# Moving the copy of the activation's high part from ScalarE to VectorE in the first three groups of a fused attention and SiLU-MLP kernel

## The chip, the cores and the metric

One core of a Trainium2 chip. The metric is the device time of one execution in microseconds; the kernel before has a median of 951.65 over three runs (951.26 to 954.59). TensorE multiplies, VectorE, ScalarE and GpSimd do the elementwise work, and SyncE's queue starts the transfers. In rows of a profile the engines are PE (PEld is its weight load), DVE, ACT, POOL and SP.

## The reference, cut to what matters

Windowed attention (8 batches, 8 heads, 576 positions of width 64, window 128, a bias per head that falls with distance), then an MLP on the 4608 tokens:

```python
x = attn_out.transpose(0, 2, 1, 3).reshape(B * S, H * D)     # 4608 x 512
h = x @ w_in                                                 # 512 x 2048
g = h * (1.0 / (1.0 + np.exp(-h)))                           # SiLU
return (g @ w_out).astype(np.float32)                        # 2048 x 512
```

The products have to be of float32 accuracy, so each operand is split into a high and a low part and a product is made of three matmuls: high by high, high by low, low by high.

## The kernel before, in words

**Tiling.** The 4608 tokens are nine groups of 512 (`TG`). For each group the 2048 hidden columns are 16 tiles (`NF`) of 128; tile n = 16 g + f. `gemm1(n, half)` makes `h` (128 hidden columns by 512 tokens in PSUM) in two halves of six matmuls; `gemm2(n, half)` adds the tile's share to four output tiles `o`, again six matmuls a half. In groups 0 to 2 (`OUT16 = 3`) the second product's operands are float32 in TensorE's rounded form (fp32r), from group 3 on 16-bit floats.

**The activation of a tile**, in four steps that the change is about:
- `act1` (ScalarE, L647): `gt` = tanh of the scaled `h`.
- `act2` (VectorE, L652): `gt` = (`gt` + 1) times `h`, which is twice the SiLU.
- `act3`: `gh` = the high part, a rounding copy of `gt`; on ScalarE, L660 in groups 0 to 2 and L662 after.
- `act4`: `gl` = `gt` - `gh`; on GpSimd in groups 0 to 2 (L135), but on VectorE (L137) for a group's last tile; on VectorE from group 3 on (L668).

`gemm2` of the tile reads `gh` first (two matmuls) and `gl` third. `gt`, `gh` and `gl` have two buffers each.

**What sets the order.** The program is written out in order, by a table of steps. `plan[point]` holds what is to be issued at a step; the MLP loop goes through `seq`, four steps a tile (`gemm1` twice for the tile, `gemm2` twice for the one before), and at each step issues first what the plan has (`begin`), then the matmuls. `later(k, fn, n)` puts a call k steps ahead. Every engine works through its own instructions in the order in which they were issued, so an engine that waits for one instruction's input holds all that stand behind it. A tile's `act1` comes right behind its `gemm1`; the other three are put by `later`. A group's last tile goes by `turn_over`, which issues `act2` to `act4` at once, between the pieces of the next group's input (`x_parts`, L608 on ScalarE and L610 on VectorE).

**What else runs in group 0.** The attention of the next tokens runs beside the MLP: `scores` (L431, `sp`), `row_max` on VectorE (L453, `t` and `mx`), `exps` on ScalarE (L463), `p_hi` on ScalarE (L472, `hr`), `p_lo` on VectorE (L477, `hr`), a transposing transfer, `attend` (L527, `av`), `normalize` (L545 to L554, `xs`), `x_hi` and `x_lo` (L564, L137, `x`), and `v_hi` on GpSimd (L400), `v_lo` on VectorE (L406) for the values. The scores and `av` share two PSUM buffers (tag `a`), so new scores wait for `xs` of an earlier pair and `av` for `row_max`. Group 0 alone also unpacks the weights, two tiles of them per activation tile (`w_next`): ScalarE splits (`w_split1` L730, `w_low3` L737), VectorE joins (`w_join` L742, `wm`), ScalarE makes the high part (`w_hi` L752, `w`) and GpSimd the low part (`w_lo` L135, `w`). Group 2 and the end of group 1 convert weights to 16 bits on ScalarE and VectorE (L780, L786, L792).

The lines that the change and the prediction touch: L647, L652, L660 and L135/L137 (activation), L742 and L752 (weights), L477, L406, L453, L554 (attention), L700 (`gemm2`), and the calls of `later` at L979 to L981.

Of the kernel before, what the change touches and what calls it, by code (L numbers as in the profile page):

```python
# [55 lines left out]
IN16, OUT16 = 2, 3  # L56
# [20 lines left out]
def at(p):  # L77

    if p < 2 * GT:
        return STEP * (p - 2 * GT) - 18  # L80
    if p < 4 * GT:
        return CLOSE[p - 2 * GT]
    return STEP * (p - 2 * GT) - LEAD
# [3 lines left out]
def tile_window_attention_then_silu_mlp(ctx, tc, qk, qk16, v, w_in, w_out, base8, out):  # L87
    nc = tc.nc
# [487 lines left out]
    def x_transpose(cc):  # L576
        xp = ps_of("h" if cc < 2 else "a", f"xp{cc}")
        for i in range(GT):
            nc.tensor.transpose(xp[:, i * P : (i + 1) * P], xt[i][:, cc * P : (cc + 1) * P], ident)
        nc.scalar.copy(xh[:, cc], xp)  # L580
        xps[cc] = xp

    def x_low(cc):
        nc.vector.tensor_sub(xl[:, cc], xps.pop(cc), f32(xh[:, cc]))
# [13 lines left out]
    def x_send():  # L598

        for i in [i for i in whole if i // GT <= now[0] + 1]:  # L600
            whole.remove(i)
            x_dma(i)
# [41 lines left out]
    def act1(n):  # L644
        gt = pool.tile([P, TG], F32, tag="gt", name=f"gt{n}")
        scale = 0.5 / W_SCALE if n // NF < IN16 else gsc[n // NF][:, 0:1]
        nc.scalar.activation(gt, hps[n], AF.Tanh, scale=scale)  # L647
        gact[n] = gt
# [5 lines left out]
    def act3(n):  # L654
        gt = gact[n]
        dt = F32R if n // NF < OUT16 else F16
        gh = pool.tile([P, TG], dt, tag="gh", name=f"gh{n}")
        gl = pool.tile([P, TG], dt, tag="gl", name=f"gl{n}")
        if n // NF < OUT16:
            nc.scalar.copy(gh, gt)  # L660
        else:
            nc.scalar.activation(gh, gt, AF.Copy, scale=CUT)  # L662
        gact[n] = (gh, gl, gt)
# [8 lines left out]
    def turn_over(n):  # L672

        i = (n // NF + 1) * GT
        more = n // NF + 1 < IN16
        if more:
            x_parts(i, 0)
        act2(n)
        act3(n)
        act4(n)  # L680
        if more:
            x_parts(i, 1)
            for k in range(1, GT):
                x_parts(i + k, 0)
                x_parts(i + k, 1)

    def gemm2(n, half):
        g, f = divmod(n, NF)
        for ti in (2 * half, 2 * half + 1):
            if f == 0:  # L690
                ops[ti] = psum.tile([P, DM], F32, tag="wxyz"[ti], name=f"o{g}_{ti}")
            gh, gl, _ = gact[n]
            t = slice(ti * P, (ti + 1) * P)
            if g < OUT16:
                hi, lo = weight("woh", f), weight("wol", f)
            else:
                hi, lo = w16[1, f][:, 0], w16[1, f][:, 1]
            seq = [(gh, hi), (gh, lo), (gl, hi)]
            for i, (a, w) in enumerate(seq):
                nc.tensor.matmul(  # L700
                    ops[ti], a[:, t], w, start=(f == 0 and i == 0), stop=(f == NF - 1 and i == len(seq) - 1),
                    skip_group_check=True,
                )
# [100 lines left out]
    def put(point, fn, *a):  # L804
        plan.setdefault(max(point, at(0)), []).append((fn, a))

    for p in range(NPAIR):
        i, q = divmod(p, 2)
        n = at(p)
# [65 lines left out]
    for b in range(1, NBB):  # L875

        n = at(2 * GT * (NBLK * b // GT)) + 2
# [11 lines left out]
    def later(n, fn, *a):  # L889
        put(pos[0] + n, fn, *a)  # L890
# [19 lines left out]
    def begin():  # L910
        for fn, a in plan.pop(pos[0], []):
            fn(*a)

    with tc.manual_schedule():
# [39 lines left out]
        for g in range(NG):  # L954
            now[0] = g

            seq = []
            for f in range(NF):
                n = g * NF + f
                seq += [("g1", n, 0)] + [("xt", 0, 2), ("xt", 0, 3)] * (n == 0) + [("g1", n, 1)]  # L960
                if 0 < f < NF - 1:
                    seq += [("g2", n - 1, 0), ("g2", n - 1, 1)]
            n = g * NF + NF - 1
            seq += [("g2", n - 1, 0), ("g2", n - 1, 1), ("g2", n, 0), ("g2", n, 1)]
            for k, n, half in seq:
                if k == "xt":
                    x_transpose(half)
                    x_low(half)
                    continue
                begin()  # L970
                x_send()
                if k == "g1":
                    gemm1(n, half)
                    if half == 1:
                        act1(n)
                        if n % NF == NF - 1:
                            turn_over(n)
                        else:
                            later(1, act2, n)  # L979
                            later(2, act3, n)  # L980
                            later(2, act4, n)  # L981
                else:
                    gemm2(n, half)
                    if n % NF == NF - 1:
                        store(g, 2 * half)
                        store(g, 2 * half + 1)
                if g == 0 and half == (n == 0):
                    w_next()
                pos[0] += 1
# [44 lines left out]
```

## Time and profile before

| | |
|---|---|
| median of three runs | 951.65 us (951.26 to 954.59) |
| the profiled execution | 949.61 us, its span 947.8 us |
| busy in the span | PE 97%, DVE 69%, ACT 59%, POOL 14% |
| the copy that moves (L660) | 48 times, 29.4 us on ACT, mean 613 ns |
| groups 0, 1, 2 | about 48 to 167, 167 to 274 and 274 to 380 us of the span |

Busy shares are means over stages: GpSimd works nearly only in groups 0 to 2, and ScalarE and VectorE are much fuller in group 0 than the mean says. A wait in a row is the idle time of an engine ahead of an instruction, with the instruction that ended it.

### The profile page before, as it was taken

Reading aid. Unit: us, or ns where it says so; the run is one execution under the profiler, and the core shown is the slowest. Engines: PE = TensorE matmul, PEld = TensorE weight load, DVE = VectorE, ACT = ScalarE, POOL = GpSimd, SP = SyncE. Lnnn points to the kernel's source line nnn. Section 1 sums busy time; section 2 is a strip of 40 time slices with the busy share of each in tenths; the row PEclk is TensorE's granted clock in tenths of the full one; section 3 lists DMA queues with packets and bytes.
Section 4 is the critical chain, followed back from the end, with each engine's and each line's share of the span. In section 5 each row is a group of like instructions: output and inputs, shape, how many; then the busy total and the mean of one; then the engine's idle time right before and its main releaser. Section 6 shows DMA issues by size and latency. Waiting matters only on the chain.

```text
span 947.8 us, 17110 instructions
## 1 busy us (share of the span) xinstructions
PE 921.9 (97%) x6442; PEld 574.9 (61%) x6442; DVE 655.0 (69%) x1603; ACT 558.9 (59%) x1152; POOL 133.5 (14%) x122
## 2 busy tenths in 40 slices
PE   8799999999999999999999999999999999999998
PEld 7677777777778888555545555555555545554443
DVE  4687887555778887899687778776777777743222
ACT  5678888676555674666567756555655565532222
POOL 0145665121212221000000000000000000000000
PEclk9999999999999999999999999999999999999999
DMA  9949942423277762644597765544654554421001
GB/s 277 375 119 246 272 101 67 106 65 87 65 181 200 166 142 50 156 101 101 111 244 179 221 144 132 118 112 98 139 111 104 119 142 106 87 55 56 1 1 44
DMA packets 209266, 123.28 MB, mean 130 GB/s; under 512 B 172576, under 2 KB 180768, under 8 KB 209184
## 3 DMA queue, kind: packets, MB, share of 16 engines
q1 hardware_dynamic: 209184, 122.19, 51.9%
q8 instruction: 50, 0.82, 0.4%
q14 instruction: 32, 0.26, 0.1%
HBM read 72.35 MB, written 9.44 MB: 86 GB/s over the span
## 4 chain that ended last, share of the span: by engine, by line
PE 78%; ACT 5%; DVE 5%; issue 2%; DMA 1%; POOL 1%; SPq 0%; DVEq 0%; ACTq 0%; POOLq 0%
PE o L700 34%; PE h L634 29%; PE h L639 6%; PE av L527 4%; PE sp L424 3%; PE sp L431 2%; DVE wm L742 1%; ACT t L463 1%; DVE t L453 1%; DVE gt L652 1%; ACT gt L647 1%; DVE x L137 1%; ACT wr L737 1%; ACT hr L472 1%; DVE v L406 1%
## 5 line engine op out<-in xcount | busy, mean ns | idle before, releaser
L700 PE MATMUL o<-w,gh 128*128 128x512 f16 (+1 forms) x1152 | 351.2, 386 | 1.4 <-ACT gh L660 1.4
L634 PE MATMUL h<-xt,w 128*128 128x512 f16 (+1 forms) x1536 | 310.6, 353 | 0.0
L647 ACT ACTIVATE gt<-h,gsc 128x512 f32<-128x512 f32 x112 | 77.0, 688 | 259.9 <-PE h L634 257.6
L700 PE MATMUL o<-w,gl 128*128 128x512 f16 (+1 forms) x576 | 221.8, 385 | 2.7 <-POOL gl L135 1.5
L634 PEld LDWEIGHTS <-w 128*128 128x128 f16 x1536 | 144.5, 98 | 125.8 <-issue 2.2
L652 DVE SCALAR_TENSOR_TENSOR gt<-gt,h 128x512 f32<-128x512 f32 x144 | 98.6, 685 | 122.6 <-ACT gt L647 122.1
L700 PEld LDWEIGHTS <-gh 128*128 128x128 f16 x768 | 74.8, 98 | 88.7
L463 ACT ACTIVATE t<-t,mx 128x256 f32<-128x256 f32 (+1 forms) x288 | 121.2, 487 | 12.3 <-DVE mx L453 12.1
L477 DVE SCALAR_TENSOR_TENSOR hr<-t,hr 128x512 f16<-128x512 f32 (+1 forms) x128 | 94.6, 741 | 23.5 <-ACT hr L472 23.3
L668 DVE SCALAR_TENSOR_TENSOR gl<-gt,gh 128x512 f16<-128x512 f32 x96 | 66.4, 692 | 53.9 <-ACT gh L662 51.3
L639 PE MATMUL h<-xh,w 128*128 128x512 f32 x256 | 90.0, 405 | 0.0
L400 POOL TENSOR_SCALAR v<-rv,vsc 128x512 f16<-128x512 f32 x30 | 24.4, 814 | 446.1 <-DMA rv<-v 233.1
L135 POOL TENSOR_TENSOR gl<-gt,gh 128x512 fp32r<-128x512 f32 x45 | 60.2, 1337 | 189.0 <-ACT gh L660 154.7
L700 PEld LDWEIGHTS o<-w,gh 128*128 128x128 f32 x384 | 69.9, 188 | 16.6 <-ACT gh L660 1.8
L472 ACT ACTIVATE hr<-t 128x512 f16<-128x512 f32 (+1 forms) x128 | 76.3, 601 | 1.0 <-DMA hl<-hr 1.0
L662 ACT ACTIVATE gh<-gt 128x512 f16<-128x512 f32 x96 | 60.2, 627 | 22.1 <-DVE gt L652 20.9
L700 PEld LDWEIGHTS <-gl 128*128 128x128 f16 x384 | 37.5, 98 | 47.9 <-DVE gl L668 3.5
L527 PEld LDWEIGHTS <-hl 128*128 128x128 f16 x1464 | 51.8, 98 | 22.4 <-issue 13.0
L453 DVE CUSTOM_DVE_ANT_0 t<-sp,tab,vsc 128x256 f32<-128x256 f32 (+1 forms) x144 | 58.6, 463 | 9.2 <-PE sp L424 8.8
L527 PE MATMUL av<-v,hl 128*128 128x65 f16 (+1 forms) x1464 | 55.8, 193 | 7.1 <-DVE v L406 5.7
L137 DVE SCALAR_TENSOR_TENSOR x<-xs,x 128x256 f16<-128x256 f32 x64 | 43.9, 687 | 24.0 <-ACT x L564 23.7
L453 DVE CUSTOM_DVE_ANT_0 t<-sp,tab 128x256 f32<-128x256 f32 (+1 forms) x144 | 50.5, 401 | 13.4 <-DMA tab<-base 7.1
(130 smaller groups left out, 1026.4 us busy)
## 6 DMA issues: line engine op xcount, KB each, us to landing
r<-qk SPq DMA_DIRECT2D x36, 512.0 KB, 4.2
out<-ot SPq DMA_DIRECT2D x36, 256.0 KB, 2.5
qs<-qk SPq DMA_DIRECT2D x18, 512.0 KB, 5.7
wr<-w_in SPq DMA_DIRECT2D x16, 512.0 KB, 7.3
wr<-w_out SPq DMA_DIRECT2D x16, 512.0 KB, 6.8
rv<-v SPq DMA_DIRECT2D x30, 256.0 KB, 3.1
vm<-v SPq DMA_DIRECT2D x27, 256.0 KB, 4.1
q<-qk SPq DMA_DIRECT2D x18, 256.0 KB, 3.6
```

The costliest lines, as they stand in the source:

```text
L135: engine.tensor_sub(out, a, b)
L453: nc.vector.tensor_tensor_reduce(out=t[:, h, 2 * P - n :], in0=st[p]["sp"][h][:, u, o].rearrange("p o c -> p (o c)"), in1=tab[:, 4 * q + 2 ...
L463: nc.scalar.activation(x, x, AF.Exp, bias=st[p]["mx"][:, 2 * u + h : 2 * u + h + 1], scale=-1.0)
L472: nc.scalar.activation(split_of(p, u, hr)[:, 0], t[:, :, 2 * P - n :], AF.Copy, scale=PSCALE)
L477: nc.vector.scalar_tensor_tensor(out=hr[:, 1], in0=t[:, :, 2 * P - n :], scalar=PSCALE, in1=hr[:, 0], op0=ALU.mult, op1=ALU.subtract)
L527: nc.tensor.matmul(av[:, 2 * u + h, : rhs.shape[-1]], lhs, rhs, start=(n == 0), stop=(n == len(seq) - 1), skip_group_check=True,)
L634: nc.tensor.matmul(o, w[:, wp, cc], x, start=start and k == 0, stop=stop, skip_group_check=True)
L639: nc.tensor.matmul(hps[n], w[:, cc], x, start=(half == 0 and i == 0), stop=(half == 1 and i == len(seq) - 1), skip_group_check=True,)
L647: nc.scalar.activation(gt, hps[n], AF.Tanh, scale=scale)
L652: nc.vector.scalar_tensor_tensor(out=gt, in0=gt, scalar=1.0, in1=hps[n], op0=ALU.add, op1=ALU.mult)
L668: nc.vector.scalar_tensor_tensor(out=gl, in0=gt, scalar=CUT, in1=gh, op0=ALU.mult, op1=ALU.subtract)
L700: nc.tensor.matmul(ops[ti], a[:, t], w, start=(f == 0 and i == 0), stop=(f == NF - 1 and i == len(seq) - 1), skip_group_check=True,)
```

## The change

`act3` of the tiles of groups 0 to 2 issues the copy on VectorE, and for all tiles but a group's last it is issued at the same step as `act2`, one step sooner than before. Nothing else is edited.

```diff
         gl = pool.tile([P, TG], dt, tag="gl", name=f"gl{n}")
         if n // NF < OUT16:
-            nc.scalar.copy(gh, gt)
+            nc.vector.tensor_copy(gh, gt)
         else:
             nc.scalar.activation(gh, gt, AF.Copy, scale=CUT)
...
                             later(1, act2, n)
-                            later(2, act3, n)
+                            later(1 if g < OUT16 else 2, act3, n)
                             later(2, act4, n)
```

VectorE's list in group 0, tile 6 (`gt` and `gh` are the tile's activation, `hr` the low part of a softmax tile, `xs` a normalized output, `wm` a weight to be joined, `x` a low part). Before:

```order
L477 SCALAR_TENSOR_TENSOR hr_0_1201<-t_0_1140,hr_0_1201 128x512
L652 SCALAR_TENSOR_TENSOR gt_1214<-gt_1214,h_1164 128x512
L554 TENSOR_TENSOR xs_1240<-av_1174,r_1216 128x256
L477 SCALAR_TENSOR_TENSOR hr_1_1220<-t_1_1143,hr_1_1220 128x512
L742 SCALAR_TENSOR_TENSOR wm_0_1237<-wm_0_1237,wr_0_676 128x512
L137 SCALAR_TENSOR_TENSOR x_1259<-xs_1240,x_1259 128x256
```

The same place in the changed kernel:

```order
L477 SCALAR_TENSOR_TENSOR hr_0_1201<-t_0_1143,hr_0_1201 128x512
L652 SCALAR_TENSOR_TENSOR gt_1214<-gt_1214,h_1164 128x512
L660 CAST gh_1231<-gt_1214 128x512
L554 TENSOR_TENSOR xs_1243<-av_1174,r_1216 128x256
L477 SCALAR_TENSOR_TENSOR hr_1_1220<-t_1_1146,hr_1_1220 128x512
L742 SCALAR_TENSOR_TENSOR wm_0_1240<-wm_0_1240,wr_0_679 128x512
L137 SCALAR_TENSOR_TENSOR x_1259<-xs_1243,x_1259 128x256
```

The copy stands between the product and `xs`; the second `hr` and `wm` stand one instruction further back. ScalarE's list at the same tile before:

```order
L647 ACTIVATE gt_1214<-h_1164 128x512
L472 ACTIVATE hr_1_1220<-t_1_1143 128x512
L752 CAST w_6_1228<-wm_1_1171 128x512
L730 ACTIVATE wm_0_1237<-wr_0_676 128x512
L737 ACTIVATE wr_0_676<-wr_0_676 128x512
L660 CAST gh_1246<-gt_1214 128x512
L564 CAST x_1259<-xs_1240 128x256
L752 CAST w_8_1273<-wm_0_1237 128x512
```

And in the changed kernel:

```order
L647 ACTIVATE gt_1214<-h_1164 128x512
L472 ACTIVATE hr_1_1220<-t_1_1146 128x512
L752 CAST w_6_1228<-wm_1_1171 128x512
L730 ACTIVATE wm_0_1240<-wr_0_679 128x512
L737 ACTIVATE wr_0_679<-wr_0_679 128x512
L564 CAST x_1259<-xs_1243 128x256
L752 CAST w_8_1273<-wm_0_1240 128x512
```

The copy is gone from between the weight's split and `x`. GpSimd's list keeps its order. This is the changed kernel's from tile 6 to tile 7 (`w` are low parts of weights, `gl` those of the activation); the kernel before has the same operations in the same places:

```order
L135 TENSOR_TENSOR w_6_1228<-wm_1_1171,w_6_1228 128x512
L135 TENSOR_TENSOR gl_1232<-gt_1214,gh_1231 128x512
L135 TENSOR_TENSOR w_8_1273<-wm_0_1240,w_8_1273 128x512
L135 TENSOR_TENSOR w_7_1310<-wm_1_1282,w_7_1310 128x512
L135 TENSOR_TENSOR gl_1314<-gt_1305,gh_1313 128x512
```

So `gh` is made sooner, and GpSimd still reaches `gl` only after the weight in front of it.

## Rows read from the trace of the kernel before

**Rows 1.** Three stretches of the trace (most of group 0, then groups 1 and 2): stretch, its length, busy us (and instructions) of PE, PEld, DVE, ACT and POOL, granted clock of TensorE, share of the DMA engines, GB/s.
```profile
57.00:137.00 80.00, 76.12 (x516) 59.09 (x515) 66.69 (x146) 68.25 (x135) 51.45 (x37) 1.00 0.85 216
165.00:275.00 110.00, 108.57 (x706) 85.39 (x705) 68.32 (x168) 69.97 (x170) 22.65 (x19) 1.00 0.38 84
275.00:380.00 105.00, 103.97 (x898) 85.07 (x895) 87.28 (x199) 64.88 (x142) 23.29 (x19) 1.00 0.64 152
```

**Rows 2.** The waits of PE in 45 to 165 us (five rows) and in 165 to 275 us (the last): who waited for whom, us in total, times, the longest.
```profile
PE sp L431 <- DVE xs L554: 1.7, 2, 0.9
PE o L700 <- ACT gh L660: 1.4, 1, 1.4
PE av L527 <- DVE mx L453: 1.3, 2, 0.7
PE o L700 <- POOL gl L135: 0.9, 2, 0.6
PE av L527 <- DVE v L406: 0.8, 1, 0.8
...
PE av L527 <- DVE v L406: 1.3, 1, 1.3
```

**Rows 3.** The longest waits of DVE and of ACT in 45 to 165 us, same columns.
```profile
DVE wm L742 <- ACT wr L737: 13.2, 13, 1.9
...
ACT w L752 <- DVE wm L742: 12.4, 15, 2.1
```

**Rows 4.** Groups of instructions of the whole span: the copy that moves, a VectorE copy whose source is in PSUM, and `v_lo` (count, busy us, mean ns, idle before). The last row is one line of the program: count, shortest/median/longest ns, first and last start.
```profile
L660 ACT CAST gh<-gt 128x512 fp32r<-128x512 f32 x48 | 29.4, 613 | 9.3 <-DVE gt L652 8.8
...
L502 DVE COPY hl<-pt 128x512 f32<-128x512 f32 x6 | 4.1, 682 | 0.9 <-PE pt L495 0.9
...
L406 DVE SCALAR_TENSOR_TENSOR v<-rv,vsc,v 128x512 f16<-128x512 f32 x30 | 24.4, 814 | 0.0
...
L610 DVE TENSOR_SCALAR xl<-xt,vsc x4: 481/482/485, 163.7 to 164.9; 128x512 fp32r<-128x512 f16 x4
```

**Rows 5.** The timeline at the first tile of group 0: start us, us, engine, line, operation, in brackets the idle time before and what ended it.
```profile
52.19 0.67 DVE L652 SCALAR_TENSOR_TENSOR gt<-gt,h 128x512 f32<-128x512 f32 x1
...
54.68 0.61 ACT L660 CAST gh<-gt 128x512 fp32r<-128x512 f32 x1
...
55.34 0.72 PE L700 MATMUL o<-w,gh 128*128 128x512 f32 x2 [1.41 <-ACT gh L660]
...
56.70 0.50 PE L700 MATMUL o<-w,gl 128*128 128x512 f32 x1 [0.63 <-POOL gl L135]
```

**Rows 6.** The timeline at the third tile, GpSimd, VectorE and PE.
```profile
66.25 1.83 POOL L135 TENSOR_TENSOR w<-wm,w 128x512 fp32r<-128x512 f32 x1 [0.63 <-ACT w L752]
68.47 1.28 POOL L135 TENSOR_TENSOR gl<-gt,gh 128x512 fp32r<-128x512 f32 x1 [0.39 <-POOL w L135]
...
68.59 1.72 DVE L742 SCALAR_TENSOR_TENSOR wm<-wm,wr 128x512 int32<-128x512 int32 x1
...
75.22 1.13 PE L431 MATMUL sp<-k,q 64*128 64x128 f32 x14 [0.94 <-DVE xs L554]
```

**Rows 7.** The timeline of GpSimd and VectorE where the two run beside each other: first a reduction of VectorE, then `v_lo`, then `hr`, `wm` and `x`, each with GpSimd's instruction of that moment; and the next `v_lo`.
```profile
76.08 1.30 POOL L135 TENSOR_TENSOR w<-wm,w 128x512 fp32r<-128x512 f32 x1 [3.75 <-ACT w L752]
...
76.14 0.68 DVE L189 TENSOR_REDUCE vmx<-vm 128x1 f32<-128x512 f32 x1
...
89.73 1.30 POOL L135 TENSOR_TENSOR w<-wm,w 128x512 fp32r<-128x512 f32 x1
...
89.80 1.78 DVE L406 SCALAR_TENSOR_TENSOR v<-early,vsc,v 128x512 f16<-128x512 f32 x1
...
98.23 0.68 DVE L477 SCALAR_TENSOR_TENSOR hr<-t,hr 128x512 f16<-128x512 f32 x1
...
98.25 1.80 POOL L135 TENSOR_TENSOR w<-wm,w 128x512 fp32r<-128x512 f32 x1 [2.67 <-ACT w L752]
...
99.41 1.19 DVE L742 SCALAR_TENSOR_TENSOR wm<-wm,wr 128x512 int32<-128x512 int32 x1 [0.50 <-ACT wr L737]
...
100.01 1.74 POOL L135 TENSOR_TENSOR gl<-gt,gh 128x512 fp32r<-128x512 f32 x1
...
112.17 1.77 DVE L406 SCALAR_TENSOR_TENSOR v<-rv,vsc,v 128x512 f16<-128x512 f32 x1
```

**Rows 8.** The chain of waits, followed back from 165 us: of the four places in 68 to 138 us where it runs through the copy that moves, the first, the third and the last (start us, us, what).
```profile
77.14 0.50 ACT gh L660
...
107.14 0.51 ACT gh L660
...
130.59 0.61 ACT gh L660
```

**Rows 9.** The timeline at the turn from group 0 to group 1, VectorE and PE.
```profile
161.73 0.69 DVE L652 SCALAR_TENSOR_TENSOR gt<-gt,h 128x512 f32<-128x512 f32 x1 [1.92 <-ACT gt L647]
...
163.10 0.69 DVE L137 SCALAR_TENSOR_TENSOR gl<-gt,gh 128x512 fp32r<-128x512 f32 x1 [0.69 <-ACT gh L660]
...
166.67 0.77 PE L527 MATMUL av<-v,hl 128*128 128x64 f16 x20 [1.29 <-DVE v L406]
```

**Rows 10.** The waits of PEld for `gl` in 165 to 275 us and in 275 to 390 us, columns as in Rows 2.
```profile
PEld o L700 <- POOL gl L135: 0.6, 1, 0.6
...
PEld o L700 <- POOL gl L135: 2.1, 3, 1.1
```

## The prediction, as it stood before the result

> **What bounds the kernel now.** I read the stretches first. TensorE's granted clock is 1.00 throughout groups 0 to 2, the higher of its two levels (2.4 GHz), and PE is busy 108.57 of 110 us in group 1 and 103.97 of 105 us in group 2 [rows 1]. The change touches only these three groups, so what it can win is the time in which PE stands still there. In the 80 us that are most of group 0 PE is idle 3.9 us, while ScalarE is busy 68.25, VectorE 66.69 and GpSimd 51.45 us [rows 1]: three engines nearly full, each waiting for the others.
>
> Then the waits of PE. The five rows of group 0 add to 1.7 + 1.4 + 1.3 + 0.9 + 0.8 = 6.1 us, and the turn to group 1 has 1.3 us more [rows 2]. Only 1.4 us is a wait for the copy that moves, and 0.9 us one for the `gl` made from it; all else waits for VectorE. VectorE in turn waits 13.2 us for ScalarE's `wr`, and ScalarE 12.4 us for VectorE's `wm` [rows 3]: unpacking the weights goes back and forth between the two, and whichever is late holds both. The chain of waits from 68 to 138 us runs through this exchange and through the copy four times, at some 0.5 us each [rows 8].
>
> **The price of the copy.** Before it is 613 ns on ScalarE, 48 times, 29.4 us in all [rows 4]. VectorE has no copy between two tiles of SBUF here. Below it is the `xl` line, SBUF to SBUF, 512 elements written as fp32r: it lasts 0.48 us, but four starts in a row lie 1.2 / 3 = 0.40 us apart [rows 4]. Above it is the copy out of PSUM, 0.68 us [rows 4]. I take 0.40 us, since source, destination and output type are those of `xl`, and keep 0.68 for the range. 48 copies are then 19 us of VectorE (33 at most). ScalarE's 29 us count only where ScalarE holds somebody.
>
> **The port that VectorE and GpSimd share.** `v_lo` started at 89.80, right behind a GpSimd subtraction that ran from 89.73 to 91.03, and ended at 91.58: 1.78 us where its mean is 0.81 [rows 4, 7]. A blocked VectorE operation so ends some 0.55 us after GpSimd's. The other way, GpSimd's subtraction at 98.25, 0.02 us behind an `hr` of VectorE, took 1.80 us instead of 1.30 [rows 7]. Both have two inputs in SBUF. A reduction with one input at 76.14 ran its usual 0.68 us in the middle of a GpSimd operation [rows 7]. No row has a fast one-input copy beside GpSimd, so what it waits is bounded by nothing at all (as the reduction) and by a whole GpSimd operation, 1.30 us (as `v_lo`).
>
> The Trainium skill ("SBUF — State Buffer", section on SBUF's two separate sides) says that this port pair is an exclusive lock for a whole instruction, taken by GpSimd, and by VectorE operations with two SBUF inputs or in a two-port mode. The trace agrees on two inputs (1.78 against 0.81 us); on the copy no row here decides. By that rule the copies would take the lock as well; what this does is rival A.
>
> **The sum, part by part.**
>
> *First tile, -0.4.* The product ends at 52.86, `gh` is done on ScalarE at 55.29 and PE stood still for 1.41 us, then 0.63 us for `gl` [rows 5]. With the copy right behind the product `gh` stands at about 53.3 and `gl` some 1.3 us later, and both stalls go, 2.0 us. I do not credit them. PE's next stall, for `xs` before the scores at 75.22 [rows 6], hangs on VectorE, and an earlier PE only waits longer there. What reaches that stall is VectorE's own gain: `wm` at 68.59 waited for GpSimd's `gl`, which started at 68.47 only because `gh` came late; the weight before it ended at 68.08 [rows 6], so `wm` gains 0.4. Bounds 0 and -2.3 (all of 1.4 + 0.9).
>
> *The full part of group 0, +2.1.* Two `v_lo` 22.4 us apart (89.80, 112.17) enclose three tiles [rows 7]; 80 / 22.4 = 3.6 such rounds. In a round ScalarE leaves out one copy that lies on the chain, -0.5 [rows 8]. VectorE has three copies more. One stands between the product and `v_lo`, where VectorE had to wait for GpSimd in any case: it adds its own 0.40. One stands ahead of the `hr` that won the port by 0.02 us at 98.23 [rows 7]. 0.4 us later it loses: it waits for a GpSimd operation of 1.30 and ends at 98.25 + 1.30 + 0.55 = 100.1 instead of 98.9; `gl`, pending by then, goes ahead of `wm`, which ends near 100.1 + 1.3 + 0.55 = 101.95 instead of 100.60, +1.35. As the race is so close, I take half, +0.7. The third copy falls into VectorE's wait for `wr` and costs nothing; if that cover goes it is 0.40 more. Round: -0.5 + 0.4 + 0.7 = +0.6, times 3.6 is +2.1. Bounds: -0.5 a round if all three hide (-1.8), and +1.25 if the race is always lost (+4.5). PE's stalls behind VectorE grow by what the round grows. Queued behind the copy are `xs`, `hr`, `wm` or `v_lo`; ScalarE waits for `hr` not at all, but for `wm` each time.
>
> *The turn, -0.3.* On VectorE `gl` started 0.68 us after the product's end, behind ScalarE's copy [rows 9]; now 0.40 us, with nothing between. `v_lo`, for which PE waits 1.29 us, stands in the same row of work and gains the 0.3.
>
> *Groups 1 and 2, -1.2.* ScalarE and VectorE have room here, GpSimd is busy 22.65 of 110 us [rows 1]. PE's weight load waited four times for `gl`, 0.6 + 2.1 us [rows 10]; the gain of 0.3 as at the turn is sure each time, and 1.2 us in all is what I take between 0 and 2.7. The sixteen copies a group, 6.4 us, go into VectorE's idle time (110 - 68.32 and 105 - 87.28 us [rows 1]). If in group 2 that cover were gone, each copy would cost its 0.40.
>
> From group 3 on nothing changes. No transfer, PSUM buffer or matmul is added, and GpSimd's list keeps its order, so `gl` in group 0 can still only come after the weight ahead of it.
>
> Sum: -0.4 + 2.1 - 0.3 - 1.2 = +0.2 us. The rows are of one execution of 949.61 us (span 947.8), 2.0 us under the median; the difference is put on the median: 951.65 + 0.2, about **951.9 us**. A measurement of this kernel can tell about 0.5% from no change, so faster means under 946.9 and slower over 956.4.
>
> **Rivals.**
>
> *A, slower: the copies are caught at the shared port.* Place: group 0, the three copies of a round. It decides if a copy waits for GpSimd as `v_lo` does. Then the race is always lost (+1.25) and of the two copies besides the one ahead of `v_lo` at least one waits half to two whole GpSimd operations more, 0.65 to 2.6 in a round: 3.6 x 1.9 = 6.8 to 3.6 x 3.85 = 13.9, less the 1.9 of the other parts. The low end, +4.9, to +7 is what I believe in: 957.5. For it: GpSimd is busy 51.45 of 80 us [rows 1], VectorE 66.69, so there is little idle time left. Against: ScalarE's relief, which lets `wr` and `hr` come sooner. The Trainium skill's rule of the lock, above, speaks for this rival.
>
> *B, faster: ScalarE sets the pace of group 0.* It is the fullest there, and VectorE's 13.2 us of waiting for it [rows 3] would swallow the copies. Then the first tile's 2.3 us stay, half of the other 3.8 us of PE's waits goes [rows 2], and the turn and the later groups add 1.5: -5.7, 946.0. Against it: ScalarE waits as long for VectorE, and all those stalls name VectorE.
>
> *C: the first tile's gain stays, the rest of group 0 is even.* -2.3 - 0.3 - 1.2 = -3.8, 947.9. For it: the two stalls are the only ones on this copy. Against: the chain through VectorE behind it.
>
> *D: the change does not do what it says.* GpSimd's order is the same, so an earlier `gh` is no earlier `gl` where a weight stands ahead, and the copies hide: only the -0.4 and a part of the later groups, 951.0.
>
> **How the numbers follow.** Forecast 0.41, A 0.20, B 0.09, C 0.15, D 0.15. The likeliest is 951.9. The range, 947.0 to 958.0, takes in the forecast with the bounds of its terms (-1.8 and +4.5 for group 0), C, D and most of A; it leaves out B and the top of A, with the tails under 0.2. Faster by over 0.5%: B and a little of C, 0.10. Slower: most of A and the forecast's upper edge, 0.20. The rest, 0.70.
>
> **What the changed profile would show.** L660 as a group of VectorE, 48 times, mean 0.40 to 0.50 us; far above that, with single copies over 1 us, is A. ScalarE's busy time down by some 29 us, VectorE's up by some 20. The wait of PE for `gh` (1.4) gone, and its waits for `gl` in groups 1 and 2 mostly gone. In group 0 the distance of `v_lo` to `v_lo` 22.4 to 23.6 us; under 22 is B or C, over 24 is A. PE's waits for `xs`, `mx` and `v` there longer than 3.8 us in all; shorter would prove my middle term wrong, as would waits of PE for something new in group 2, where I put nothing.

## The result, and the profile after

The changed kernel takes **957.6 us** (median of six runs, 956.58 to 958.47); the kernel before, on the same chip, 951.72 (951.26 to 954.59, six runs). The ratio is 1.0055 [1.0043, 1.0066], or 4.1 to 6.3 us more. The forecast was 951.9: the time lies inside the range given, close to its upper end, and on the figure of rival A, but the likeliest case was wrong: by the prediction's own limit (slower over 956.4) this is the outcome to which it gave 0.20. The range held through its upper bounds, not through the forecast. Below, a ratio is turned into us on 952 us, so the change is +5.2.

The first line of the changed kernel's page gives the busy time of each engine.

```profile
PE 927.2 (97%) x6442; PEld 580.7 (61%) x6442; DVE 669.2 (70%) x1651; ACT 533.7 (56%) x1104; POOL 137.6 (14%) x122
```

The three stretches of [rows 1], in the changed kernel:

```profile
57.00:137.00 80.00, 72.28 (x493) 55.97 (x492) 68.47 (x151) 60.87 (x122) 49.28 (x35) 1.00 0.84 208
165.00:275.00 110.00, 108.68 (x691) 85.32 (x690) 69.29 (x184) 61.65 (x152) 28.35 (x23) 1.00 0.39 85
275.00:380.00 105.00, 103.65 (x886) 85.31 (x885) 90.80 (x211) 56.55 (x125) 24.17 (x19) 1.00 0.70 159
```

In the 80 us of group 0 ScalarE is busy 60.87 instead of 68.25 us, and that buys nothing: VectorE goes from 66.69 to 68.47, and PE loses 3.8 us, 72.28 for 76.12. In groups 1 and 2 PE is as busy as before.

**Reading two single profiles against each other needs care at the start.** The span after is 8.9 us longer, more than the medians differ. Here are 34 to 45 and 45 to 57 us of the kernel before, and then of the changed one (columns as in [rows 1]):

```profile
34.00:45.00 11.00, 7.64 (x50) 7.00 (x50) 5.48 (x18) 5.39 (x12) 1.82 (x2) 0.84 1.06 390
45.00:57.00 12.00, 9.42 (x54) 6.90 (x54) 7.92 (x21) 6.90 (x15) 1.63 (x2) 1.00 0.17 65
```

```profile
34.00:45.00 11.00, 7.88 (x36) 7.06 (x36) 5.34 (x16) 5.15 (x11) 1.70 (x2) 0.56 1.05 390
45.00:57.00 12.00, 12.00 (x60) 10.22 (x61) 5.48 (x18) 2.74 (x6) 0.00 (x0) 0.69 0.10 38
```

The granted clock was 0.56 and 0.69 where it had been 0.84 and 1.00, and the first tile's tanh starts 4.4 us later. The first copy that the change moves starts at 57.1 us, so this is not its work. I therefore read distances within the MLP: the starts of tanh of tiles 1, 16 and 47, which stand for the start and the end of group 0 and the end of group 2, before and after.

```profile
55.71 0.60 ACT L647 ACTIVATE gt<-h 128x512 f32<-128x512 f32 x1
...
171.81 0.60 ACT L647 ACTIVATE gt<-h 128x512 f32<-128x512 f32 x1 [2.96 <-PE h L639]
...
373.88 0.69 ACT L647 ACTIVATE gt<-h,gsc 128x512 f32<-128x512 f32 x1 [4.14 <-PE h L634]
```

```profile
59.58 0.58 ACT L647 ACTIVATE gt<-h 128x512 f32<-128x512 f32 x1
...
181.12 0.60 ACT L647 ACTIVATE gt<-h 128x512 f32<-128x512 f32 x1 [2.96 <-PE h L639]
...
383.16 0.69 ACT L647 ACTIVATE gt<-h,gsc 128x512 f32<-128x512 f32 x1 [5.33 <-PE h L634]
```

Group 0 takes 121.54 us instead of 116.10, **+5.4**, which is the whole loss. Groups 1 and 2 take 202.04 instead of 202.07: nothing. Nor is the loss spread evenly over group 0. From one start of tanh to another, tile 2 to tile 5 takes 2.1 us more than before, 5 to 8 0.5, 8 to 11 0.1, 11 to 14 1.9, and 14 to 16 0.9.

Now the waits of 45 to 170 us in the changed kernel, first PE's, then those between VectorE and ScalarE; they answer to [rows 2, 3].

```profile
PE sp L431 <- DVE xs L554: 4.7, 5, 1.6
PE av L527 <- DVE mx L453: 3.1, 3, 2.1
...
PE o L700 <- POOL gl L135: 1.4, 2, 0.9
PE av L527 <- DVE v L406: 1.4, 1, 1.4
...
ACT w L752 <- DVE wm L742: 18.8, 16, 2.9
...
DVE wm L742 <- ACT wr L737: 8.9, 9, 1.9
```

PE's wait for `gh` is gone. Its waits for VectorE (`xs`, `mx`, `v`) are 9.2 us instead of 3.8. The give and take over the weights has turned round: VectorE waits 8.9 us for ScalarE (13.2 before), ScalarE 18.8 us for VectorE (12.4 before). Of ScalarE's relief 6.4 us ended as longer waiting for VectorE.

The copy's line in the changed kernel, beside [rows 4]: count, shortest, median and longest ns.

```profile
L660 DVE CAST gh<-gt x48: 426/427/1416, 57.1 to 384.6; 128x512 fp32r<-128x512 f32 x48
```

Alone it takes 0.427 us, close to the 0.40 taken. Those of up to 1.42 us are copies that run into GpSimd. In group 0 the 16 copies hold VectorE 11.45 us, not 16 x 0.427 = 6.8. One such place is tile 12. The same place in the kernel before first, then in the changed one:

```profile
141.99 0.66 DVE L652 SCALAR_TENSOR_TENSOR gt<-gt,h 128x512 f32<-128x512 f32 x1
142.51 1.74 PE L431 MATMUL sp<-k,q 64*128 64x128 f32 x16
142.52 1.28 POOL L135 TENSOR_TENSOR w<-wm,w 128x512 fp32r<-128x512 f32 x1 [1.30 <-ACT w L752]
142.56 0.42 DVE L554 TENSOR_TENSOR xs<-av,r 128x256 f32<-128x256 f32 x1
```

```profile
149.36 0.66 DVE L652 SCALAR_TENSOR_TENSOR gt<-gt,h 128x512 f32<-128x512 f32 x1
149.90 1.28 POOL L135 TENSOR_TENSOR w<-wm,w 128x512 fp32r<-128x512 f32 x1 [1.28 <-ACT w L752]
...
150.05 1.40 DVE L660 CAST gh<-gt 128x512 fp32r<-128x512 f32 x1
151.38 0.41 DVE L554 TENSOR_TENSOR xs<-av,r 128x256 f32<-128x256 f32 x1
...
151.93 1.13 PE L431 MATMUL sp<-k,q 64*128 64x128 f32 x14 [1.55 <-DVE xs L554]
```

GpSimd's low part of a weight starts as VectorE's product ends, in both kernels (142.52, 149.90). Before, the next on VectorE was `xs`, which has one of its inputs in PSUM and was not held up. Now the copy stands there, waits GpSimd out, and `xs` and with it the scores come 1.4 to 1.5 us later: PE, which did not stand still here, stands still for 1.55 us. The Trainium skill ("SBUF — State Buffer", section "SBUF: two separate sides") names a float32 copy between two tiles of SBUF as one that takes both ports and locks GpSimd out, and its rule of the lock, told in the prediction, lets such a copy wait in turn. The trace now agrees: 1.40 against 0.43 us. Of the four copies that stand ahead of `xs` (tiles 3, 6, 9 and 12) only this one was caught; the others took 0.43.

The other long stall is at tile 2. This is `hr` there in the kernel before, then the same place in the changed one:

```profile
66.22 0.68 DVE L477 SCALAR_TENSOR_TENSOR hr<-t,hr 128x512 f16<-128x512 f32 x1
```

```profile
69.52 0.43 DVE L660 CAST gh<-gt 128x512 fp32r<-128x512 f32 x1
...
70.01 1.75 POOL L135 TENSOR_TENSOR w<-wm,w 128x512 fp32r<-128x512 f32 x1 [0.62 <-DVE gh L660]
...
70.52 1.78 DVE L477 SCALAR_TENSOR_TENSOR hr<-t,hr 128x512 f16<-128x512 f32 x1
...
73.88 0.89 PE L527 MATMUL av<-v,hl 128*128 128x65 f16 x24 [2.09 <-DVE mx L453]
```

Before, `hr` started 0.03 us ahead of GpSimd's weight (66.25, [rows 6]) and took 0.68 us. Now the copy stands ahead of it, with `v_lo` between. The copy itself is not held up, but `hr` starts 0.51 us behind GpSimd and takes 1.78. `row_max` stands behind it, and PE waits 2.09 us for `mx`, where it did not wait before. These two stalls lie in the two stretches that lose about 2 us each.

Copies are also caught ahead of `v_lo`. There the change moved a wait rather than made one: the three `v_lo` from 97 to 144 us last 0.74 us ([rows 7] has 1.78 and 1.77, and the next of the kernel before, first here, 1.77). The changed kernel's stand second:

```profile
135.73 1.77 DVE L406 SCALAR_TENSOR_TENSOR v<-rv,vsc,v 128x512 f16<-128x512 f32 x1
```

```profile
97.03 0.74 DVE L406 SCALAR_TENSOR_TENSOR v<-early,vsc,v 128x512 f16<-128x512 f32 x1
120.08 0.74 DVE L406 SCALAR_TENSOR_TENSOR v<-rv,vsc,v 128x512 f16<-128x512 f32 x1
144.16 0.74 DVE L406 SCALAR_TENSOR_TENSOR v<-rv,vsc,v 128x512 f16<-128x512 f32 x1
```

They lie 23.0 and 24.1 us apart, where the kernel before has 22.4 and 23.6.

A third thing is `hr`, which now stands further back and meets GpSimd more often. Its line in group 0, before (57 to 172 us) and after (59 to 182 us):

```profile
L477 DVE SCALAR_TENSOR_TENSOR hr<-t,hr 128x512 f16<-128x512 f32 x20 | 16.3, 813 | 3.7 <-ACT hr L472 3.7
```

```profile
L477 DVE SCALAR_TENSOR_TENSOR hr<-t,hr 128x512 f16<-128x512 f32 x20 | 21.2, 1059 | 3.8 <-ACT hr L472 3.6
```

One `hr` lasts 1.06 us in the mean instead of 0.81; ten of the 20 last over 1.1 us, where three did.

### The profile page after: what moved, and what is told of

The parts are those of the page before. It is cut to its first block, busy times and chain, and to the rows that moved or that the text cites. A ratio compares the mean times of both kernels' runs of the same rounds, so it can differ in the third digit from the quotient of the medians.

```text
span 956.7 us, 17130 instructions
## 1 busy us (share of the span) xinstructions
PE 927.2 (97%) x6442; PEld 580.7 (61%) x6442; DVE 669.2 (70%) x1651; ACT 533.7 (56%) x1104; POOL 137.6 (14%) x122
## 4 chain that ended last, share of the span: by engine, by line
PE 78%; DVE 7%; ACT 4%; issue 3%; DMA 1%; SPq 0%; POOL 0%; DVEq 0%; ACTq 0%; POOLq 0%
PE o L700 34%; PE h L634 29%; PE h L639 6%; PE av L527 4%; PE sp L424 3%; PE sp L431 2%; DVE wm L742 1%; DVE hr L477 1%; DVE gt L652 1%; ACT t L463 1%; ACT wm L730 1%; DVE v L406 1%; DMA hl<-hr 1%; ACT wr L737 1%; ACT gt L647 0%
## 5 line engine op out<-in xcount | busy, mean ns | idle before, releaser
L135 POOL TENSOR_TENSOR gl<-gt,gh 128x512 fp32r<-128x512 f32 x45 | 65.9, 1464 | 181.9 <-DVE gh L660 172.2
L639 PEld LDWEIGHTS h<-xh,w 128*128 128x128 f32 x256 | 48.7, 190 | 12.2 <-issue 0.2
```

Source lines behind the costliest of these rows:

```text
L135: engine.tensor_sub(out, a, b)
L639: nc.tensor.matmul(hps[n], w[:, cc], x, start=(half == 0 and i == 0), stop=(half == 1 and i == len(seq) - 1), skip_group_check=True,)
```

## The experiments

Twelve kernels, each against the kernel before on the same chip. Distances from tile to tile are from one profile of each kernel. **P** is the theory that the loss is the copies' waiting for GpSimd, **V** that it is VectorE's time however it is spent, **Q** that it is the place ahead of `xs`, `hr` and `wm`.

### Where: group 0, or the later ones

Group 0 keeps ScalarE's copy; groups 1 and 2 are as changed.

```diff
-        if n // NF < OUT16:
+        if n // NF == 0:
+            nc.scalar.copy(gh, gt)
+        elif n // NF < OUT16:
             nc.vector.tensor_copy(gh, gt)
...
-                            later(1 if g < OUT16 else 2, act3, n)
+                            later(1 if 0 < g < OUT16 else 2, act3, n)
```

> Group 0 as before (ScalarE copies, one step later), groups 1 and 2 as in the change. Theory P (the copies of group 0 meet GpSimd at the port that it shares with VectorE), V (any 16 copies more are too much for VectorE's full list in group 0) and Q (it is their place, ahead of xs, hr and wm) all say that the loss lies in group 0: 950.5 to 952.0, that is before minus 0 to 1.2. If the loss came from the later groups or from something that the change does to the whole program, it stays near 957.

Measured: 951.68 us, ratio 0.9997 [0.9983, 1.0012]. The loss lies in group 0, and the other 32 copies neither win nor lose, as the distances of the two profiles said.

### Which half of the change: the engine or the step

VectorE with the old, later step (first line), and ScalarE with the new, earlier step (second):

```diff
-                            later(1 if g < OUT16 else 2, act3, n)
+                            later(2, act3, n)
```

> The copy on VectorE, but at the later step of before. P and V: the same 48 copies on the same engine, 956 to 959, as the change. Q: with the copy behind xs and hr of its step the loss goes, 951.5 to 953.5.

```diff
-            nc.vector.tensor_copy(gh, gt)
+            nc.scalar.copy(gh, gt)
```

> The copy on ScalarE as before, but at the earlier step of the change. P and V: VectorE is as before, so 950 to 953, with the wait of PE for the first gh shorter. Q: a copy that goes ahead of older work costs on ScalarE too, 953.5 to 957.

Measured: VectorE at the later step 959.91 us, 1.0079 [1.0055, 1.0103]; ScalarE at the earlier step 953.05, 1.0010 [0.9996, 1.0023]. So the move to VectorE makes the loss, and the earlier step on ScalarE isn't shown to cost anything. The later step on VectorE doesn't cure the whole, but it doesn't leave the loss where it was. The copy then stands behind `xs`, `hr` and `row_max`. Its copies hold VectorE 12.89 us in group 0, more than the change's 11.45, and yet tile 1 to tile 16 takes 117.89 us, +1.8 where the change has +5.4. These are PE's waits for `xs` and `mx` in 45 to 170 us, nearly those of [rows 2] again:

```profile
PE sp L431 <- DVE xs L554: 2.4, 3, 0.9
...
PE av L527 <- DVE mx L453: 0.7, 2, 0.5
```

The rest of this kernel's loss lies elsewhere. Tile 16 to tile 47 takes 4.1 us more, and at the start of group 2 PE has a stall that the change does not have, the longest in 280 to 395 us (in 290 to 294 us the granted clock was then 0.62):

```profile
PE o L700 <- DVE gh L660: 3.0, 1, 3.0
```

Q missed the time, 951.5 to 953.5, but in group 0 its mechanism shows: the place counts. The profile is of an execution of 956.65 us; the kernel's others took up to 962.17, and where those lose more is not known.

### A copy that does not wait for GpSimd

The copy as a reduction over a last axis of length one, which has one input:

```diff
-            nc.vector.tensor_copy(gh, gt)
+            nc.vector.tensor_reduce(gh, gt.rearrange("p (t o) -> p t o", o=1), axis=AX.X, op=ALU.max)
```

> The change, with the copy made by a VectorE reduction over a last axis of length one: the same place and result, one input, no fast mode (0.68 us in place of 0.43). P: no copy waits for GpSimd any more (longest under 0.8 us, where the change has six of 16 at 0.87 to 1.42 in group 0), and the time is 953 to 957, not above the change. V: 16 x 0.25 = 4 us more of VectorE in group 0, 960 to 963.

Measured: 957.53 us, 1.0060 [1.0036, 1.0083]. The line of the copy, and tile 12 in this kernel:

```profile
L660 DVE TENSOR_REDUCE gh<-gt x48: 685/686/690, 54.1 to 382.5; 128x512 fp32r<-128x512 f32 x48
```

```profile
146.65 1.27 POOL L135 TENSOR_TENSOR w<-wm,w 128x512 fp32r<-128x512 f32 x1 [1.28 <-ACT w L752]
...
146.81 0.69 DVE L660 TENSOR_REDUCE gh<-gt 128x512 fp32r<-128x512 f32 x1
147.41 0.41 DVE L554 TENSOR_TENSOR xs<-av,r 128x256 f32<-128x256 f32 x1
...
147.97 1.13 PE L431 MATMUL sp<-k,q 64*128 64x128 f32 x14 [0.82 <-DVE xs L554]
```

No copy is ever held up, and the whole loss is about the same. But it is not the same loss. From tile 1 to 5 this kernel loses 3.2 us (the change 2.0), from tile 5 to 16 1.1 (3.5), and from tile 16 to 47 2.2 us, where the change loses nothing. That the sums agree is chance, as far as one profile each tells; neither forecast was hit, P's 953 to 957 nor V's 960 to 963. At tile 12 PE's stall is 0.82 us where the copy lasts 0.69; it was 1.55 where the copy lasted 1.40. At tile 2 it is the operations behind the copy that now wait for GpSimd, `v_lo` (1.74 us) and then `hr`, and PE stands still for 3.25 us for `mx`:

```profile
68.67 1.75 DVE L477 SCALAR_TENSOR_TENSOR hr<-t,hr 128x512 f16<-128x512 f32 x1
```

P in its pure form, that only the copies' own waiting costs, falls: without any of it group 0 loses 4.3 us. That waiting for GpSimd costs, whichever of VectorE's operations it hits, is not ruled out by this kernel. V is not shown by it either: the 16 copies take 10.98 us of VectorE, the plain ones with their waits 11.45, but the losses lie in different places.

### No copy, and twice the copy

In group 0 the product is written in the rounded form and used as `gh`:

```diff
-        gh = pool.tile([P, TG], dt, tag="gh", name=f"gh{n}")
+        gh = gt if n // NF == 0 else pool.tile([P, TG], dt, tag="gh", name=f"gh{n}")
...
-        if n // NF < OUT16:
+        if n // NF == 0:
+            pass
+        elif n // NF < OUT16:
             nc.vector.tensor_copy(gh, gt)
```

> The change without the copy in group 0: the product is written in the rounded form and serves as its own high part, so the low part becomes zero (this leaves out the split of the activation there; every other instruction stays). ScalarE keeps its relief of 16 copies and VectorE pays nothing. Theory V (what counts is the time that the copies hold VectorE in group 0, some 11 us, at about half a us of the end for each): the loss is gone, 949.5 to 952. Theory P (only the waiting at the port with GpSimd costs): the same, 950 to 952, since no copy is left to wait. Theory R (the loss comes from ScalarE's instructions that now stand closer together, and not from VectorE): 956 to 958, as the change. If it lies under 950.5, ScalarE's relief alone is worth something; at 951.7 it is worth nothing.

```diff
             nc.vector.tensor_copy(gh, gt)
+            if n // NF == 0:
+                nc.vector.tensor_copy(gh, gt)
```

> The change with the copy made twice on VectorE in group 0, one right behind the other into the same tile. V: 16 more copies of 0.43 us, some of them held up, are 7 to 11 us more of VectorE, at half a us each +3.5 to +5.5 over the change: 961 to 963. P: the second copy stands where the first has already got the port, so it seldom waits, and only the low part comes 0.43 us later: 958 to 959.5. R: 957 to 958.

Measured: no copy 948.92 us, 0.9953 [0.9936, 0.9971], -4.5 us; the copy twice 968.37, 1.0158 [1.0137, 1.0180], +15.0. So with neither engine making the copy the kernel is 4.5 us faster than before. That is ScalarE's relief together with a `gh` that is there with the product and a `gl` that can start sooner; this kernel does not part them. Against it VectorE's copies cost 9.7, and 16 more of them another 9.8. R (ScalarE's order) falls. So does P's forecast for the double copy: the second copies hold VectorE 9.74 us themselves, as three of them wait although they follow a copy directly. V was right in direction and too low in size (961 to 963), and not all of the last 9.8 us is VectorE's time: in this kernel's profile the clock fell after four stalls of PE (last section).

### GpSimd out of the way

The weights' low parts are left out in two kernels, the change and the one with ScalarE's copy in group 0:

```diff
-        w = weights[key][:, int(part)]
+        w = weights[key][:, 0]
...
-        minus(nc.gpsimd, lo, wraw.pop((f, which))[1], f32(hi))
+        wraw.pop((f, which))
```

> The change with GpSimd's subtractions for the weights left out (the high part of a weight stands in for its low part, so the weights' low parts are left out); GpSimd then has in group 0 only one subtraction a tile and the values. To be read against the next kernel, which is the same with ScalarE's copy in group 0. VectorE's other instructions also meet GpSimd less, so both may be faster than the kernel before: 940 to 951. P: the two are within 1 us of each other. V: VectorE still has 16 x 0.43 = 6.9 us more, so this one is 2.5 to 4 us slower than the other, unless VectorE now has idle time enough to hide them; its idle time in 57 to 137 us tells which. R: 5 to 6 us slower than the other.

> The reference of the run with GpSimd's weight subtractions left out: the same, with ScalarE's copy a step later in group 0 (groups 1 and 2 as in the change). P, V and R: 940 to 951 by what GpSimd cost VectorE before; it gives the zero for the other. If VectorE's waits at the port were worth nothing to the whole, it stays at 951 to 952.

Measured: VectorE's copy 948.82 us, 0.9957 [0.9940, 0.9973]; ScalarE's 946.30, 0.9934 [0.9917, 0.9952]. The group of the copies in 45 to 180 us of the first (18 of them, two of group 1):

```profile
L660 DVE CAST gh<-gt 128x512 fp32r<-128x512 f32 x18 | 7.7, 427 | 0.9
```

Every copy now takes its 0.427 us, 6.84 us in group 0, and the loss shrinks from 5.5 (change against ScalarE's copy in group 0, 1.0055 - 0.9997) to 2.2 us (0.9957 - 0.9934), though the intervals of the last two overlap a little. So GpSimd has a part in the loss, some 3 of 5.5 us. The two profiles say more: from tile 0 to tile 16 they differ by only 0.6 us (117.44 and 116.83), where the change and ScalarE's copy in group 0 differ by 4.6 (125.59 and 121.02); the rest of the 4.0 us between the spans of the first two lies ahead of tile 0, where no copy stands yet. Whether GpSimd costs by lengthening the copies or the operations behind them is not parted here, since its weights are out of the way of both. V had said 2.5 to 4, P under 1 and R 5 to 6: R falls, and between V and P the pair does not decide.

### Half of the copies, and less for VectorE in another way

Even tiles of group 0 back on ScalarE, at its later step:

```diff
-        if n // NF < OUT16:
+        if n // NF < OUT16 and (n // NF or n % 2):
             nc.vector.tensor_copy(gh, gt)
+        elif n // NF < OUT16:
+            nc.scalar.copy(gh, gt)
```

> The change, with every second copy of group 0 (those of even tiles) back on ScalarE at its later step; groups 1 and 2 as in the change. Theory V (each us for which a copy holds VectorE in group 0 puts the end off by 0.8 to 0.9 us, less 0.35 us for each us that ScalarE is rid of): half the copies, half the loss, +2.5 to +3.5 over the kernel before, 954 to 955.5. Rival S (VectorE has idle time for some of the copies, and only the last ones cost): under half, +0 to +1.5, 952 to 953.5. Rival P2 (it is the copies that meet GpSimd, 6 of 16, that cost): between, by how many of the eight are held up.

The low part of the normalized outputs on GpSimd in group 0, once in the kernel before and once in the changed one:

```diff
-            minus(nc.vector, xt[i][:, 1, cols], st[p]["x"], xt[i][:, 0, cols])
+            minus(nc.gpsimd if now[0] < 1 else nc.vector, xt[i][:, 1, cols], st[p]["x"], xt[i][:, 0, cols])
```

> The kernel before, with another 8 operations taken from VectorE in group 0: the low parts of the normalized outputs (L137, x) are subtracted by GpSimd there. V: VectorE is rid of 8 x 0.88 = 7.0 us; at 0.8 to 0.9 that is -6, less what GpSimd's 8 operations more (some 0.7 us each) hold VectorE up by, at most 5.6 us x 0.85: -1 to -5, 947 to 951. S: VectorE's time was idle time in any case: 951.5 to 953.

> The change with the same 8 operations moved from VectorE to GpSimd in group 0. V: as much less as the kernel before gains by it, or a little more since VectorE is fuller: 952 to 956.5. S: most of the loss is gone, 951.5 to 953. If it is no faster than the change (957.6), what counts is neither VectorE's time nor its idle time but the port alone.

Measured: half of the copies 952.80 us, 1.0001 [0.9987, 1.0016]; `x` on GpSimd in the kernel before 953.31, 1.0006 [0.9992, 1.0021]; in the changed one 957.29, 1.0039 [1.0023, 1.0056]. V as a straight line falls twice: eight copies hold VectorE 6.58 us and cost nothing, as S said, and eight operations less for VectorE in the kernel before win nothing. The second has a reason in its profile. This is the line of `wm` in 45 to 176 us, before and then with `x` on GpSimd:

```profile
L742 DVE SCALAR_TENSOR_TENSOR wm<-wm,wr 128x512 int32<-128x512 int32 x29 | 26.0, 895 | 15.4 <-ACT wr L737 13.2 <-issue 2.2
```

```profile
L742 DVE SCALAR_TENSOR_TENSOR wm<-wm,wr 128x512 int32<-128x512 int32 x29 | 30.0, 1036 | 16.9 <-ACT wr L737 13.4 <-issue 2.2 <-POOL x L135 1.2
```

Of the roughly 7 us taken off VectorE 4.0 came back as longer waits of `wm` for GpSimd, and the rest did not reach PE. In the changed kernel the move takes the ratio from 1.0055 to 1.0039; the intervals overlap, so that is open.

### Number or place

Only the four copies right ahead of `xs` (tiles 3, 6, 9 and 12) go back to ScalarE, at its later step:

```diff
-        if n // NF < OUT16:
+        if n // NF < OUT16 and n not in (3, 6, 9, 12):
             nc.vector.tensor_copy(gh, gt)
+        elif n // NF < OUT16:
+            nc.scalar.copy(gh, gt)
```

> The change, with four copies of group 0 back on ScalarE at its later step: those of tiles 3, 6, 9 and 12, which stand on VectorE right ahead of xs, the operation that PE's new waits name most. Twelve copies stay on VectorE. Theory N (number: what counts is how many copies VectorE holds; 8 cost nothing and 16 cost 5.9): 12 lie between, +2 to +4 over the kernel before, 954 to 956. Theory W (where: the four ahead of xs make the loss, the others only free ScalarE): the loss is gone, -2 to +0.5, 950 to 952.8, and it may beat the kernel before.

Measured: 954.01 us, 1.0013 [1.0000, 1.0025], +1.2. Neither theory's range was hit: not the 2 to 4 us of N, nor the 0.5 at most of W. Four copies of sixteen make 4.0 of the 5.2 us, and PE's wait for `xs` is back at the 1.7 us of [rows 2], while that for `mx` stays as in the change (45 to 170 us):

```profile
PE av L527 <- DVE mx L453: 3.1, 3, 2.1
...
PE sp L431 <- DVE xs L554: 1.6, 2, 0.8
```

Side by side; the last three columns are differences from the kernel before in its distances from tile to tile (31.65, 84.45 and 202.07 us), of one profile each:

| copies on VectorE in group 0 | they hold it, us | whole, us on 952 [interval] | tile 1 to 5 | 5 to 16 | 16 to 47 |
|---|---|---|---|---|---|
| 0, none at all | 0 | -4.5 [-6.1, -2.8] | -0.2 | -2.2 | 0.0 |
| 0, all 16 on ScalarE | 0 | -0.3 [-1.6, 1.1] | +0.4 | -0.1 | 0.0 |
| 0, on ScalarE a step sooner | 0 | +1.0 [-0.4, 2.2] | +1.3 | +1.7 | -0.8 |
| 8, the others on ScalarE | 6.58 | +0.1 [-1.2, 1.5] | +1.2 | +0.3 | 0.0 |
| 12, the four at `xs` on ScalarE | 8.47 | +1.2 [0.0, 2.4] | +1.9 | +1.3 | 0.0 |
| 16, the change | 11.45 | +5.2 [4.1, 6.3] | +2.0 | +3.5 | 0.0 |
| 16, a step later | 12.89 | +7.5 [5.2, 9.8] | +1.5 | +0.3 | +4.1 |
| 16 as reductions | 10.98 | +5.7 [3.4, 7.9] | +3.2 | +1.1 | +2.2 |
| 32 | 20.56 | +15.0 [13.0, 17.1] | +5.7 | +13.2 | 0.0 |

These distances move with the clock: a part of group 0 ran at the lower level in the profiles of the 8, the 12 and the 32 copies and of ScalarE's sooner step, but none of it from tile 1 to 16 in the others. The time for which VectorE is held is not the measure. From eight copies to the change it is 5.1 us for 4.9, but from none on VectorE to eight 0.4 for 6.6; and the 16 copies of the later step hold it longest of all the kernels with 16 and cost 1.8 us in group 0. Place is the better reading: copies that go ahead of `xs`, and of the `hr` ahead of the row maxima, cost, and copies behind them cost little in group 0. It rests on two kernels, this one, whose whole time is near that of the kernel before, and the later step, by one profile. How much of the cost is the copy's own 0.43 us, and how much the waiting for GpSimd that it brings on, is not shown, and no kernel has VectorE's copy at the later step in group 0 alone. No kernel tried that computes the same is faster than the one before.

## Why the prediction was right or wrong

**What bounds the kernel** held: PE's stalls in group 0 behind VectorE, and the exchange of `wr` and `wm`.

**The price of the copy** was right: 0.427 against 0.40 us alone. What it meets was bounded by 0 and 1.30 us, and 1.42 - 0.43 = 1.0 was seen.

**First tile, -0.4.** The size came, the mechanism did not. Tile 0 to tile 1 of the tanh is 4.05 us instead of 4.54, -0.5, and every kernel without ScalarE's copy at tile 0 has 4.01 to 4.06, every other one 4.53 to 4.67. But the term was worked out at the third tile, where `wm` was to end 0.4 sooner. Counted from tile 1's tanh that `wm` ended at 14.60 us before and ends at 15.10 now: it takes 0.69 us instead of 1.72, as `gl` is out of its way, but the `hr` ahead of it has lost its race. That the two sizes agree is luck.

**The full part of group 0, +2.1: this step failed.** From tile 1 to tile 16 +5.4 us were measured. What failed first is the factor, 3.6 equal rounds. The round was forecast at +0.6, and where its rows were read it grew by 0.7 and 0.5 (`v_lo` to `v_lo`); by the tanh, tile 5 to 8 and 8 to 11 grew by 0.5 and 0.1. Tile 2 to 5 and 11 to 14 grew by 2.1 and 1.9, each with one long stall of PE (2.09 us for `mx`, 1.55 for `xs`) that has no term in the sum. In the terms of a round:
- The lost race was the right kind of cost, and I had halved it as a toss. In the two rounds where it was read it was lost both times: `hr` took 1.43 us at 104.88 and at 128.52, and the `wm` behind it 1.77. Since these rounds grew by no more than forecast, another of their terms must have been better than its price; which one is not shown. At tile 2, where `hr` had won by as little, losing it made the stall of 2.09 us.
- The copy ahead of `xs` got no price of its own, although [rows 2] name `xs` as PE's longest wait: at tile 12 PE's stall grew by the whole length of the copy. GpSimd's weight starts there as VectorE's product ends, before and after.
- VectorE's three copies were 0.4 + 0.7 + 0 a round, 4.0 us; from no copy to the change it is 9.7 us (0.9953 to 1.0055). The third was to fall into VectorE's wait for `wr`, 13.2 us long; that wait sank by only 4.3 us while 16 copies took 11.45.
- ScalarE's relief, -0.5 a round or -1.8, was not measured alone. Without any copy in group 0 the kernel is 4.5 us faster, with the first tile and an earlier `gh` and `gl` in it.

**The turn, -0.3**, was right in kind: `gl` starts 0.49 us after the product's end (0.68 before, 0.40 forecast), and PE's wait for `v_lo` there fell from 1.29 to 1.10 us.

**Groups 1 and 2, -1.2.** PE's weight load waited four times for `gl`, and these waits fell from 2.7 to 1.3 us; but tile 16 to tile 47 takes 202.04 instead of 202.07 us, and ScalarE's copy in group 0 with VectorE's after it gives -0.3 [-1.6, 1.1]. Nothing came: a wait of the weight load that lies beside a busy PE was credited as time. The slip was to read PEld's waits as PE's.

**Rival A** had the right time, and the right sign that would show it, single copies over 1 us. Its reason, copies that wait at the port, was a part of it: with GpSimd's weights gone the loss falls to 2.2 us or less, but a copy that never waits and is 0.26 us longer still loses 4.3 us in group 0, where operations behind it wait instead. **Rival B** may have named something real, as the kernel without any copy is 4.5 us faster, and had the copies' cost wrong. **C and D** fell with group 0.

**The signs.** ScalarE's busy time -25.2 (forecast -29), VectorE's +14.2 (+20). Both engines' instructions differ by just 48, so no record is missing; ScalarE's -25.2 is 0.53 us a copy, near the 0.50 that one took on the chain [rows 8] rather than the mean of 0.61 [rows 4]. Copies in group 0 0.72 us in the mean, outside 0.40 to 0.50; the distance of `v_lo` 23.0 and 24.1, a weak sign, as the limits were set from one distance of 22.4 and the kernel before has one of 23.6 itself; PE's waits for VectorE 9.2 us, far over 3.8. A stall for something new in group 2, where nothing was put, came: 0.9 us for `vsc` at L280, without an effect on the distance.

## What to carry to other kernels

Work that is moved between two engines which wait for each other is priced by what stands right behind it in the list, instruction by instruction: a copy ahead of an operation that PE waits for can cost its whole length, one in a wait that exists anyway can cost nothing, and the busy shares (83% against 85% here) tell neither. It need not be the moved piece that is slowed: a copy of 0.43 us made the `hr` behind it lose the port, and that cost 1.1. So look for the places where two engines are nearly even, and do not carry a round read in one place over a whole stretch. Two kernels with the same total need not have the same loss: compare them stretch by stretch before a theory is dropped. A wait of the weight load is time only where the matmuls stop as well.

## What the runs showed of the hardware

Beside GpSimd's subtractions a VectorE copy from SBUF to SBUF (fp32r from float32, 128x512) takes 0.43 to 1.42 us (1.51 in the kernel with the later step), a reduction over an axis of one, with the same result, always 0.685 to 0.690.

Stalls of PE can cost a second time, through the clock. The kernel with two copies has a stall of 3.33 us for `mx` that ends at 74.3; the stretches around it are these:

```profile
71.00:75.00 4.00, 0.70 (x19) 0.73 (x20) 3.90 (x13) 0.91 (x2) 1.18 (x1) 0.96 0.28 54
75.00:78.00 3.00, 3.00 (x16) 2.42 (x14) 1.64 (x5) 2.87 (x6) 1.29 (x1) 0.50 0.97 256
```

The granted clock stood at its lower level (0.50, 1.2 GHz) right after, while PE was busy throughout. Three later stretches of this profile, each behind a stall too, have 0.72:

```profile
108.00:114.00 6.00, 5.54 (x27) 4.60 (x28) 5.57 (x14) 2.19 (x4) 2.56 (x2) 0.72 0.70 178
...
136.00:142.00 6.00, 6.00 (x26) 4.62 (x26) 4.65 (x15) 3.17 (x7) 1.29 (x1) 0.72 0.63 178
...
160.00:166.00 6.00, 5.90 (x28) 5.00 (x29) 4.09 (x12) 2.41 (x5) 2.35 (x2) 0.72 0.01 3
```

If PE's work was slower there as its clock, that is some 6 us in the four stretches, an estimate from these rows, of the 13.4 us by which this profile's tile 1 to 16 is longer than the change's. In the kernel with twelve copies a stall of 2.09 us at the same place was followed by 0.55 in 72 to 74 us; in the changed kernel's profile a stall of 2.10 us there was followed by 1.00. So a like stall brings the clock down in one execution and not in another; whether that adds to the change's loss in its other runs isn't shown, as only one of them has a profile. The same holds for the start: after PE's wait of 3.6 us that ends at 37 to 38 us, in all kernels, the lower level lasted past 50 us in the changed kernel's profile and till about 42 in that of the kernel before.
